# Windowed attention into an ELU feed-forward on one core: values 3 and 4 loaded ahead of w_in's second quarter, and batch 2's k transposed by DMA

## The chip, the core and the metric

The kernel runs on one core of a Trainium2 chip. TensorE does matmuls and transposes into PSUM, VectorE (DVE) and ScalarE (ACT) do elementwise work, GpSimd (POOL) builds masks and issues the loads that convert float32 to bfloat16, SyncE (SP) issues other transfers. The metric is the device time of one execution in microseconds. The kernel before took 306.71 us, the median of 3 runs (306.45 to 306.94).

## The reference

Two parts, joined. Attention in 8 batches of 8 heads, 576 positions of 64 numbers, in which each query sees only the keys within 32 positions; then a feed-forward over the 4608 x 512 result with an ELU between two matrix products.

```python
def _attn_ref(q, k, v):
    scores = (1.0 / np.sqrt(D)) * np.matmul(q, k.transpose(0, 1, 3, 2))
    mask = np.abs(pos[:, None] - pos[None, :]) <= 32
    scores = np.where(mask, scores, -1000000000.0)
    scores = scores - np.max(scores, axis=-1, keepdims=True)
    attn = np.exp(scores)
    attn = attn / (np.sum(attn, axis=-1, keepdims=True) + 1e-09)
    return np.matmul(attn, v)

def _moe_ref(x, w_in, w_out):          # x 4608x512, w_in 512x2048, w_out 2048x512
    h = x @ w_in
    g = np.where(h > 0.0, h, np.exp(np.minimum(h, 0.0)) - 1.0)
    return g @ w_out
```

## The kernel before

The feed-forward runs in 144 steps, eight for each tile of 256 tokens (the first two tiles take turns). Step kk does a first product `mm1(kk)`, its exponential `e_sb` on ScalarE, `m_sb = e_sb - 1`, and one step later `elu(kk)` on VectorE; the second product `mm2` follows two steps behind. Attention is laid between: it is done in pairs of 64-query blocks, 36 pairs, and each part of a pair is filed under a step and a slot of it ("first", "dve", "mid", "end").

```python
def at(kk, slot, fn, *args):
    tasks.setdefault((kk, slot), []).append((fn, args))
...
LAG = 2
for kk in range(NSTEP + LAG):
    run(kk, "first")
    if 1 <= kk < NSTEP and kk != 3:
        elu(kk - 1)
    run(kk, "dve")
    if kk < NSTEP:
        mm1(kk)
    run(kk, "mid")
    for n in {2: (), 3: (), 4: (), 5: (2, 3)}.get(
            kk, (kk - LAG,) if kk >= LAG else ()):
        mm2(n)
    run(kk, "end")
```

`mm1` alternates between two PSUM tiles h0 and h1, so that step kk can't begin before `elu(kk - 2)` has read the older one:

```python
def mm1(kk):
    t, s = order[kk]
    h = kk % 2
    ...                                       # ps: PSUM tile h0 or h1, 8 matmuls
        nc.scalar.activation(e_sb, ps, AX.Exp)
        if 1 <= kk <= 3:
            nc.scalar.activation(m_sb, e_sb, AX.Copy, bias=-1.0)
        else:
            nc.vector.tensor_scalar(m_sb, e_sb, -1.0, None, ALU.add)
```

A pair goes through `scores` (16 matmuls, TensorE), `exponential` (ScalarE), `mask` (VectorE), `pv` (product with the values, TensorE), `normalize` (VectorE), `x_transpose` (TensorE) and `x_evac` (a copy to xT, ScalarE). The values of a batch lie in five overlapping tiles of 128 positions (`load_v(b, 0..4)`, "values 3" is tile 3); `rotate_v` copies halves of them into a second layout for odd query blocks. Both tiles 3 and 4 are needed for pairs 2 and 3 of batch 0. `idle(n, tag)` runs n matmuls on zeros, as a filler that keeps TensorE active.

w_in comes in four quarters of its columns, w_out in four quarters of its rows. Steps 0 and 1 use w_in's first quarter, steps 2 and 3 its second, `mm2(0)` and `mm2(1)` w_out's first. The loads of GpSimd's queue in the front:

```python
for which in range(2):
    load_cast(0, which, HALF_B)      # q and k of batch 0, second half
load_w_in(0)
...                                  # two masks
load_w_in(1)
for m in (3, 4):
    load_v(0, m)
load_w_out(0)
load_w_out(1)
```

Pairs 2 and 3, which xT of the second token tile (steps 4 to 7) waits for:

```python
at(0, "mid", scores, 2, "s")
at(0, "mid", scores, 3, "u")
for i in (2, 3):
    at(0, "mid", exponential, i)
    at(1, "dve" if i == 2 else "mid", mask, i)
    at(3, "dve", rotate_v, 0, 2, VS - 1, (i - 2,))
    at(3, "mid", pv, i)
at(1, "mid", idle, 3, "y1")
at(3, "dve", idle, 3, "y1")
...                                  # normalize, elu(2), mm2(0), mm2(1), transposes, all in step 3
```

q and k come in float32 with head pairs on the free axis, are cast to bfloat16 and must be turned so that the 128 numbers of two heads lie on the partitions. There are two ways. One is on TensorE: 9 transposes of 128x128 into PSUM and one copy out of it, by ScalarE. The other is through DRAM: the cast rows are written there and come back through a transposing DMA.

```python
def cast_qk(b, which, part, j0, n, eng): ...      # float32 -> bfloat16, n of 18 columns
def transpose_qk(b, which, part, j0, n, evac, tag="t0", later=None):
    pt = ps_tile([128, 1024 if n <= 8 else 2048], BF16, tag, "ptx")
    for j in range(n):
        nc.tensor.transpose(pt[:, j * 128:(j + 1) * 128],
                            qk_b[b, which, z][:, j0 + j, :], ident)
    ...                                           # evac copies pt to qT or kT
def write_rows(b, which):
    nc.scalar.dma_start(out=..., in_=...)         # cast rows to DRAM, ScalarE's queue
def transpose_rows(b, which):
    nc.sync.dma_start_transpose(out=keys_or_queries(b, which),
                                in_=in_dram.pop((b, which)))
```

Batches 3 to 7 go through DRAM, batch 2 through TensorE: casts in steps 18 (VectorE), 20, 21 (ScalarE) and 23 (VectorE), transposes in steps 22 to 25. Step 26 is the first that needs them. The outputs of token tiles 0 and 1 leave PSUM in steps 16 and 17, one half by ScalarE and one by VectorE (`y_sb`), and pair 7's scores in step 18 ("u") lie in the two banks of tile 1's outputs:

```python
def mm2(kk):
    if s == 0:
        psY[t] = [ps_tile([128, D_MODEL], FP32, g, "psY")
                  for g in (("h2", "t0") if t == 1 else ("y0", "y1"))]
    ...
    if s == STEPS - 1:
        for ts in range(2):
            eng = (nc.scalar, nc.vector)[z]
            copy_on(eng, y_sb, psY[t][ts])
...
at(BACK_AT, "dve", swap_back)        # BACK_AT = 18: h2 and t0 become "u" again
```

`hold_v(b)` is a tiny VectorE write into the values' tile, so that the loads of batch b wait for VectorE's step.

Of the kernel before, what the change touches and what calls it, by code (L numbers as in the profile page):

```python
# [21 lines left out]
def kernel(  # L22
# [9 lines left out]
    nc = tc.nc  # L32
# [14 lines left out]
    VS = 5  # L47
# [9 lines left out]
    NSTEP = NT * STEPS  # L57
# [54 lines left out]
    WHOLE, HALF_A, HALF_B = (0, SJ), (0, SJ // 2), (1, SJ // 2)  # L112
    qk_f = {}

    def load_qk(b, which, part, engs=(nc.sync, nc.sync)):
        z, nj = part
        t = lpool.tile([128, 2, nj * D], FP32, tag=f"f{which}{nj}",
                       name=f"f{which}")
        qk_f[b, which, z] = t
        src = (q, k)[which][b, :, z * NC * nj:(z + 1) * NC * nj, :].rearrange(  # L120
            "(g h) (c j) d -> c g h (j d)", h=2, j=nj)
        for h in range(2):
            engs[h].dma_start(out=t[:, h, :], in_=src[:, :, h, :])
# [14 lines left out]
    def load_v(b, m):  # L138
        lo = 128 * m - WIN
        p0 = max(0, -lo)  # L140
        p1 = min(128, S - lo)
        nc.gpsimd.dma_start(  # L142
            out=V_e[b % 3][p0:p1, m, :, 0:D],
            in_=v[b, :, lo + p0:lo + p1, :].rearrange("h p d -> p h d"))
# [28 lines left out]
    def load_w_in(c):  # L173
        w = D_FF // 4
        nc.gpsimd.dma_start(  # L175
            out=w_in_sb[:, :, c * w:(c + 1) * w],
            in_=moe_w_in[:, c * w:(c + 1) * w].rearrange(
                "(o p) f -> p o f", p=128))

    def load_w_out(c):  # L180
        n = NFO // 4
        nc.gpsimd.dma_start(
            out=w_out_sb[:, c * n:(c + 1) * n, :],
            in_=moe_w_out[c * n * 128:(c + 1) * n * 128, :].rearrange(
                "(o p) f -> p o f", p=128))
# [191 lines left out]
    def first_pair(b):  # L377
        return NQB * b // 2
# [27 lines left out]
    for mi in (0, 4):  # L406
# [4 lines left out]
        out=masks[:, 3, :], in_=masks[:, 3, :], compare_op=ALU.is_ge,  # L411
        fill=0.0, base=128 - WIN - 1, pattern=[[0, QB]],
        channel_multiplier=-1)
    load_w_in(1)
    for m in (3, 4):
        load_v(0, m)
    load_w_out(0)
    load_w_out(1)

# [38 lines left out]
    gate(w_in_at(3))  # L458
    for which in range(2):
        load_qk(1, which, HALF_B)  # L460
    for which in range(2):
        load_qk(2, which, WHOLE)


# [4 lines left out]
    def at(kk, slot, fn, *args):  # L469
        tasks.setdefault((kk, slot), []).append((fn, args))  # L470

    def run(kk, slot):
        for fn, args in tasks.get((kk, slot), ()):
            fn(*args)
# [11 lines left out]
    at(0, "mid", scores, 3, "u")  # L486
    for i in (2, 3):
        at(0, "mid", exponential, i)
        at(1, "dve" if i == 2 else "mid", mask, i)
        at(3, "dve", rotate_v, 0, 2, VS - 1, (i - 2,))  # L490
        at(3, "mid", pv, i)

    at(1, "mid", idle, 3, "y1")
    at(3, "dve", idle, 3, "y1")
    for i in (2, 3):
        at(3, "mid", normalize, i)
    at(3, "mid", lambda: elu(2))
    for i in (2, 3):
        at(3, "mid", lambda n: mm2(n), i - 2)
        at(3, "mid", x_transpose, i)  # L500
        at(3, "mid", x_evac, i, nc.scalar)
    at(4, "dve", swap_pools)

    for part, kq in ((HALF_A, 7), (HALF_B, 15)):
# [20 lines left out]
    for i in range(4, NPAIR):  # L525
        two = i >= FIRST_TWO
        kk, z = begin[i], i % 2 if two else 0
# [5 lines left out]
        n = kk + (3 + z if two else 2)  # L533
# [9 lines left out]
    for b in range(2, B):  # L543
        k0 = begin[first_pair(b)]


        l_qk, l_v, c0 = {2: (0, 0, 0), 3: (15, 24, 22), 4: (35, 36, 41),
                         5: (52, 52, 57), 6: (68, 68, 73),
                         7: (84, 84, 89)}[b]
        if b >= 3:  # L550
            at(l_qk, "end", load_qk, b, 0, WHOLE)
            at(l_qk, "end", load_qk, b, 1, WHOLE)
            if b > 3:
                at(l_v, "dve", hold_v, b)
            for m in range(VS):
                at(l_v + m, "mid", load_v, b, m)
        if b <= 3:
            at((21, 28)[b - 2], "mid", rotate_v_dma, b)
        else:
            for n, back in enumerate((10, 8, 3, 2)):  # L560
                m0 = 2 * (n // 2)
                at(k0 - back, "dve", rotate_v, b, m0, m0 + 2, (n % 2,))
        if b == 2:

            for n, (which, j0) in enumerate(((0, 0), (0, 9), (1, 0), (1, 9))):
                at((18, 20, 21, 23)[n], ("mid", "end", "end", "mid")[n],
                   cast_qk, b, which, WHOLE, j0, 9,
                   (nc.vector, nc.scalar, nc.scalar, nc.vector)[n])
                at(22 + n, "end" if n == 1 else "mid", transpose_qk, b, which, WHOLE, j0, 9,
                   nc.scalar, "su"[n % 2])  # L570
            continue


        free = [f for f in range(c0, k0) if f not in starts]
        for n, (which, j0) in enumerate(
                (which, j0) for which in range(2) for j0 in (0, 6, 12)):
            at(free[n], "end", cast_qk, b, which, WHOLE, j0, 6,
               nc.vector if free[n] < 26 else nc.scalar)
            if j0 == 12:
                at(free[n], "end", write_rows, b, which)  # L580
                at(free[n] + (3 if free[n] == 29 else 4), "mid",
                   transpose_rows, b, which)
# [8 lines left out]
# [5 lines that stand above are left out]
        tags = (f"h{h}", "s") if kk == NSTEP - 1 else (f"h{h}",)  # L596
        w = FG // len(tags)
        psH[kk], m_t[kk] = [], []
        for z, tag in enumerate(tags):
            ps = ps_tile([128, w, TT], FP32, tag, "ps")  # L600
            psH[kk].append(ps)
            for j in range(w):
                fo = s * FG + z * w + j
                for do in range(NDO):
                    nc.tensor.matmul(  # L605
                        ps[:, j, :],
                        lhsT=w_in_sb[:, do, fo * 128:(fo + 1) * 128],
                        rhs=xT[t][:, :, do, :],
                        start=(do == 0), stop=(do == NDO - 1))
        for z, ps in enumerate(psH[kk]):  # L610
            e_sb = mpool.tile([128, w, TT], FP32, tag="e_sb", name="e_sb")
            nc.scalar.activation(e_sb, ps, AX.Exp)  # L612
            m_sb = mpool.tile([128, w, TT], BF16, tag="m_sb", name="m_sb")
            if 1 <= kk <= 3:

                nc.scalar.activation(m_sb, e_sb, AX.Copy, bias=-1.0)
            else:
                nc.vector.tensor_scalar(m_sb, e_sb, -1.0, None, ALU.add)  # L618
            m_t[kk].append(m_sb)
            if kk == NSTEP - 1:  # L620
                elu(kk, z)

    def elu(kk, z=0):
        if z == 0:
            g_t[kk] = mpool.tile([128, FG, TT], BF16, tag="g_sb", name="g_sb",
                                   bufs=5)
        ps = psH[kk][z]
        w = ps.shape[1]
        nc.vector.scalar_tensor_tensor(  # L629
            g_t[kk][:, z * w:(z + 1) * w, :], ps, 0.0, m_t[kk][z],  # L630
            ALU.max, ALU.min)
# [3 lines left out]
# [5 lines that stand above are left out]
        g_sb = g_t.pop(kk)  # L640
        last = t == NT - 1 and s == STEPS - 1
        for ts in range(2):
            for j in range(FG):
                nc.tensor.matmul(  # L644
                    psY[t][ts],
                    lhsT=g_sb[:, j, ts * 128:(ts + 1) * 128],
                    rhs=w_out_sb[:, s * FG + j, :],
                    start=(s == 0 and j == 0),
                    stop=(s == STEPS - 1 and j == FG - 1))
        if s == STEPS - 1:  # L650
            for ts in range(2):
                z = 1 - ts if last else ts
                eng = (nc.scalar, nc.vector)[z]
                y_sb = opool.tile([128, D_MODEL], FP32, tag=f"y_sb{z}",
                                  name="y_sb")
                copy_on(eng, y_sb, psY[t][ts])
                (nc.scalar if last and ts else nc.sync).dma_start(
                    out_t[t, :, ts, :], y_sb)

    LAG = 2  # L660
    for kk in range(NSTEP + LAG):
        run(kk, "first")
        if 1 <= kk < NSTEP and kk != 3:
            elu(kk - 1)
        run(kk, "dve")
        if kk < NSTEP:
            mm1(kk)
        run(kk, "mid")

        for n in {2: (), 3: (), 4: (), 5: (2, 3)}.get(  # L670
                kk, (kk - LAG,) if kk >= LAG else ()):
            mm2(n)
        run(kk, "end")
# [30 lines left out]
```

The softmax here doesn't subtract the row's maximum and nothing guards it: scores larger than these inputs give would overflow.

## Time and profile before

| What | Value |
|---|---|
| time, median of 3 runs | 306.71 us |
| span of the profiled execution | 304.7 us |
| TensorE busy | 294.7 us (97%) |
| VectorE busy | 240.7 us (79%) |
| ScalarE busy | 170.3 us (56%) |
| granted TensorE clock | 1.000 |
| one group of a step's first product, from start to start of the next | 0.87 us |
| first matmul of step 4 | 25.42 us |
| first matmul of step 18 | 55.06 us |

A row of the timeline gives the start of an instruction (or a run of equal ones), the us that it spans, the engine, the source line, what is written from what with the shape, and in brackets the idle time of the engine ahead of it with what ended that. Where one instruction overlaps the next a little, the distance from start to start is the cost, and not the span. L605 is `mm1`, L644 `mm2`, L395 a filler, L304 `scores`, L336 `pv`, L279 a transpose of q or k, L357 a transpose of x, L612 the exponential, L618 and L616 m_sb, L629 `elu`, L234 and L236 copies and casts by ScalarE and VectorE. "us to landing" is from the issue of a transfer to its completion. In the list of DMA queues q0 is GpSimd's, q1 SyncE's, q10 ScalarE's.

### The profile page before, as it was taken

What the parts mean: (1) busy time and instruction counts of PE and PEld (TensorE: products, weight loads), DVE (VectorE), ACT (ScalarE), POOL (GpSimd) and SP (SyncE); (2) the same over time, 40 slices, a digit from 0 to 9 for tenths busy, and PEclk for the clock granted to TensorE, in tenths of its full rate; (3) what the DMA queues carried; (4) which work ended last, traced back from release to release, by engine and by line L of the source; (5) the groups of instructions that cost most, each with busy time, mean ns of one, the idle gap of its engine ahead of it and who ended that gap; (6) DMA issues with size and microseconds to landing.
All of it is one profiled execution on the core that took longest, in us unless ns stands there. A gap on an engine that the chain in (4) does not pass through costs nothing.

```text
span 304.7 us, 7633 instructions
## 1 busy us (share of the span) xinstructions
PE 294.7 (97%) x3090; PEld 197.0 (65%) x3090; DVE 240.7 (79%) x470; ACT 170.3 (56%) x256; POOL 48.7 (16%) x68
## 2 busy tenths in 40 slices
PE   7799999999999999999999999999999999999994
PEld 3466666677666666666666666666666666666662
DVE  6866587978788887988798879887988787877663
ACT  3673556778664567546754675467545454543431
POOL 8836100910004100230023002300000000000000
PEclk9999999999999999999999999999999999999999
DMA  9999999999766997999799969996911111121011
GB/s 192 189 193 206 182 268 397 309 154 207 167 187 154 297 120 208 225 325 152 154 265 309 183 161 267 321 160 150 269 34 71 34 71 34 72 37 69 8 63 70
DMA packets 91973, 52.81 MB, mean 173 GB/s; under 512 B 76578, under 2 KB 81698, under 8 KB 91938
## 3 DMA queue, kind: packets, MB, share of 16 engines
q1 hardware_dynamic: 47186, 35.48, 43.6%
q0 software_dynamic: 42880, 10.10, 43.2%
q10 hardware_dynamic: 1872, 6.75, 5.7%
q8 instruction: 24, 0.39, 0.5%
q14 instruction: 11, 0.09, 0.1%
HBM read 36.70 MB, written 15.34 MB: 171 GB/s over the span
## 4 chain that ended last, share of the span: by engine, by line
PE 89%; DMA 4%; POOL 3%; DVE 1%; ACT 1%; issue 0%; POOLq 0%; DVEq 0%
PE psY L644 41%; PE ps L605 40%; DMA w_out_sb<-in_moe_w_out_dram 4%; PE psS L336 3%; PE psS L304 3%; POOL Ve L142 1%; PE ptx L279 1%; POOL c L136 1%; PE psXT L357 1%; POOL w_in_sb L175 0%; PE ptx L274 0%; ACT pu L315 0%; DVE x_st L348 0%; DVE pm L324 0%; DVE g_sb L629 0%
## 5 line engine op out<-in xcount | busy, mean ns | idle before, releaser
L612 ACT ACTIVATE e_sb<-ps 128x512 f32<-128x512 f32 (+1 forms) x145 | 86.3, 595 | 118.0 <-PE ps L605 110.4
L605 PE MATMUL ps<-xT,w_in_sb 128*128 128x256 bf16 x1152 | 149.3, 273 | 1.8 <-ACT xT L234 0.7
L644 PE MATMUL psY<-w_out_sb,g_sb 128*128 128x512 bf16 x576 | 147.5, 379 | 0.0
L605 PEld LDWEIGHTS <-w_in_sb 128*128 128x128 bf16 x1152 | 110.5, 98 | 40.7 <-DMA w_in_sb<-in_moe_w_in_dram 1.6
L629 DVE SCALAR_TENSOR_TENSOR g_sb<-ps,m_sb 128x512 bf16<-128x512 f32 (+1 forms) x145 | 99.4, 686 | 13.3 <-DVE m_sb L618 0.5
L618 DVE TENSOR_SCALAR m_sb<-e_sb 128x512 bf16<-128x512 f32 (+1 forms) x142 | 61.2, 431 | 38.3 <-ACT e_sb L612 36.4
L644 PEld LDWEIGHTS <-g_sb 128*128 128x128 bf16 x576 | 54.5, 98 | 38.5 <-DVE g_sb L629 0.2
L142 POOL DMA_DIRECT2D Ve<-in_v_dram x40 | 35.3, 893 | 138.9 <-PE psS L336 79.9
L315 ACT ACTIVATE pu<-psS 128x1024 bf16<-128x1024 f32 x36 | 36.5, 1021 | 1.4 <-PE psS L304 1.4
L348 DVE TENSOR_TENSOR x_st<-psS,rc 128x512 bf16<-128x512 f32 x36 | 24.9, 691 | 1.2
L324 DVE TENSOR_TENSOR pm<-pu,masks 128x1024 bf16<-128x1024 bf16 x36 | 24.6, 683 | 0.7 <-ACT pu L315 0.6
L234 ACT CAST qkb<-f 128x768 bf16<-128x768 f32 (+1 forms) x29 | 24.9, 860 | 0.0
L336 PEld LDWEIGHTS <-pm 128*64 128x64 bf16 x576 | 11.0, 111 | 8.8 <-DVE pm L324 7.7
L336 PE MATMUL psS<-Ve,pm 128*64 128x65 bf16 x320 | 13.2, 196 | 0.8 <-DVE pm L324 0.7
L236 DVE COPY y_sb<-psY 128x512 f32<-128x512 f32 x18 | 12.3, 684 | 0.9 <-PE psY L644 0.9
L304 PEld LDWEIGHTS <-kT 64*128 64x128 bf16 x576 | 9.6, 95 | 4.9 <-issue 4.0
L304 PE MATMUL psS<-qT,kT 64*128 64x64 bf16 x576 | 11.8, 191 | 0.5 <-DVE kT L236 0.5
L336 PE MATMUL psS<-Vo,pm 128*64 128x65 bf16 x256 | 11.9, 196 | 0.0
L234 ACT COPY y_sb<-psY 128x512 f32<-128x512 f32 x18 | 10.5, 582 | 2.2 <-PE psY L644 2.2
L153 DVE COPY Vo<-Ve 64x1040 bf16<-64x1040 bf16 x24 | 10.4, 435 | 1.3 <-DMA Ve<-in_v_dram 0.5
L395 PE MATMUL ps_idle<-zeros 128*128 128x512 bf16 x26 | 8.3, 450 | 1.3 <-DVE zeros L194 1.3
L234 ACT COPY qT<-ptx 128x1152 bf16<-128x1152 bf16 (+2 forms) x8 | 7.5, 972 | 3.5 <-PE ptx L279 2.8
(36 smaller groups left out, 73.3 us busy)
## 6 DMA issues: line engine op xcount, KB each, us to landing
out_dram<-y_sb SPq DMA_DIRECT2D x35, 256.0 KB, 3.7
f<-in_q_dram SPq DMA_DIRECT2D x12, 576.0 KB, 6.1
f<-in_k_dram SPq DMA_DIRECT2D x12, 576.0 KB, 8.2
in_dram<-qkb ACTq DMA_DIRECT2D x10, 576.0 KB, 4.5
Ve<-in_v_dram POOLq DMA_DIRECT2D x24, 128.0 KB, 11.4
w_in_sb<-in_moe_w_in_dram POOLq DMA_DIRECT2D x4, 512.0 KB, 9.8
w_out_sb<-in_moe_w_out_dram POOLq DMA_DIRECT2D x4, 512.0 KB, 12.5
Ve<-in_v_dram POOLq DMA_DIRECT2D x16, 96.0 KB, 10.3
```

The costliest lines, as they stand in the source:

```text
L142: nc.gpsimd.dma_start(out=V_e[b % 3][p0:p1, m, :, 0:D], in_=v[b, :, lo + p0:lo + p1, :].rearrange("h p d -> p h d"))
L234: nc.scalar.copy(d_, s_)
L304: nc.tensor.matmul(psS[:, h % 2, hp * 128 + z * QB:hp * 128 + (z + 1) * QB], lhsT=kT[b % 2][base:base + 64, KPAD + hp * S + QB * qb - WIN: ...
L315: nc.scalar.activation(pu, _bap(psS, [psS.ap[0], [1, 1024]]), AX.Exp, scale=SCALE)
L324: nc.vector.tensor_mul(pm, pu, _bap(mm, [mm.ap[0], [0, H], [1, 2 * QB]]))
L336: nc.tensor.matmul(psS[QB * z:QB * (z + 1), par, hp * VD:(hp + 1) * VD], lhsT=pm[:, par * HP + hp, z * QB:(z + 1) * QB], rhs=vv[:, qb // 2 ...
L348: nc.vector.tensor_mul(x_st, _bap(psS, [psS.ap[0], [VD, HP], [512, 2], [1, D]]), _bap(rc, [rc.ap[0], [2, HP], [1, 2], [0, D]]))
L605: nc.tensor.matmul(ps[:, j, :], lhsT=w_in_sb[:, do, fo * 128:(fo + 1) * 128], rhs=xT[t][:, :, do, :], start=(do == 0), stop=(do == NDO - 1))
L612: nc.scalar.activation(e_sb, ps, AX.Exp)
L618: nc.vector.tensor_scalar(m_sb, e_sb, -1.0, None, ALU.add)
L629: nc.vector.scalar_tensor_tensor(g_t[kk][:, z * w:(z + 1) * w, :], ps, 0.0, m_t[kk][z], ALU.max, ALU.min)
L644: nc.tensor.matmul(psY[t][ts], lhsT=g_sb[:, j, ts * 128:(ts + 1) * 128], rhs=w_out_sb[:, s * FG + j, :], start=(s == 0 and j == 0), stop=( ...
```

## The change

Four things. First, in GpSimd's queue values 3 and 4 of batch 0 come ahead of w_in's second quarter, and pairs 2 and 3 are done earlier: rotation and mask in step 0, products in step 1 between 4, 2 and 1 fillers, normalization in step 2; `mm2(0)` and `mm2(1)` come after both transposes of x in step 3, `elu(2)` comes in the ordinary place, and m_sb is on ScalarE in step 1 only. Second, k of batch 2 goes through DRAM: both casts in step 16, rows written at the end of step 16, the transposing DMA in step 18; q of batch 2 stays on TensorE. Third, batch 2's k is loaded ahead of its q, and batch 3's k at the end of step 18, behind the transposing DMA in SyncE's queue, in place of step 15. Fourth, the values of batch 3 are held until step 20; before, they followed those of batch 2 directly. The aim is to take k's transposes from TensorE and to keep the transfers of the two batches out of each other's way.

```diff
--- before.py
+++ after.py
@@ -411,9 +411,9 @@
         out=masks[:, 3, :], in_=masks[:, 3, :], compare_op=ALU.is_ge,
         fill=0.0, base=128 - WIN - 1, pattern=[[0, QB]],
         channel_multiplier=-1)
-    load_w_in(1)
     for m in (3, 4):
         load_v(0, m)
+    load_w_in(1)
     load_w_out(0)
     load_w_out(1)
 
@@ -458,7 +458,7 @@
     gate(w_in_at(3))
     for which in range(2):
         load_qk(1, which, HALF_B)
-    for which in range(2):
+    for which in (1, 0):
         load_qk(2, which, WHOLE)
 
 
@@ -486,19 +486,16 @@
     at(0, "mid", scores, 3, "u")
     for i in (2, 3):
         at(0, "mid", exponential, i)
-        at(1, "dve" if i == 2 else "mid", mask, i)
-        at(3, "dve", rotate_v, 0, 2, VS - 1, (i - 2,))
-        at(3, "mid", pv, i)
-
-    at(1, "mid", idle, 3, "y1")
-    at(3, "dve", idle, 3, "y1")
     for i in (2, 3):
-        at(3, "mid", normalize, i)
-    at(3, "mid", lambda: elu(2))
-    for i in (2, 3):
-        at(3, "mid", lambda n: mm2(n), i - 2)
+        at(0, "mid", rotate_v, 0, 2, VS - 1, (i - 2,))
+        at(0, "mid", mask, i)
+
+        at(1, "mid", idle, (4, 2)[i - 2], "y1")
+        at(1, "mid", pv, i)
+        at(2, "dve", normalize, i)
         at(3, "mid", x_transpose, i)
         at(3, "mid", x_evac, i, nc.scalar)
+    at(1, "end", idle, 1, "y1")
     at(4, "dve", swap_pools)
 
     for part, kq in ((HALF_A, 7), (HALF_B, 15)):
@@ -549,9 +546,8 @@
                          7: (84, 84, 89)}[b]
         if b >= 3:
             at(l_qk, "end", load_qk, b, 0, WHOLE)
-            at(l_qk, "end", load_qk, b, 1, WHOLE)
-            if b > 3:
-                at(l_v, "dve", hold_v, b)
+            at(18 if b == 3 else l_qk, "end", load_qk, b, 1, WHOLE)
+            at(20 if b == 3 else l_v, "dve", hold_v, b)
             for m in range(VS):
                 at(l_v + m, "mid", load_v, b, m)
         if b <= 3:
@@ -562,12 +558,16 @@
                 at(k0 - back, "dve", rotate_v, b, m0, m0 + 2, (n % 2,))
         if b == 2:
 
-            for n, (which, j0) in enumerate(((0, 0), (0, 9), (1, 0), (1, 9))):
-                at((18, 20, 21, 23)[n], ("mid", "end", "end", "mid")[n],
-                   cast_qk, b, which, WHOLE, j0, 9,
-                   (nc.vector, nc.scalar, nc.scalar, nc.vector)[n])
-                at(22 + n, "end" if n == 1 else "mid", transpose_qk, b, which, WHOLE, j0, 9,
-                   nc.scalar, "su"[n % 2])
+
+            for n in range(2):
+                at((18, 20)[n], ("mid", "end")[n], cast_qk, b, 0, WHOLE,
+                   9 * n, 9, (nc.vector, nc.scalar)[n])
+                at(22 + n, ("mid", "end")[n], transpose_qk, b, 0, WHOLE,
+                   9 * n, 9, nc.scalar, "su"[n])
+                at(16, "mid", cast_qk, b, 1, WHOLE, 9 * n, 9,
+                   (nc.vector, nc.scalar)[n])
+            at(16, "end", write_rows, b, 1)
+            at(18, "mid", transpose_rows, b, 1)
             continue
 
 
@@ -611,7 +611,7 @@
             e_sb = mpool.tile([128, w, TT], FP32, tag="e_sb", name="e_sb")
             nc.scalar.activation(e_sb, ps, AX.Exp)
             m_sb = mpool.tile([128, w, TT], BF16, tag="m_sb", name="m_sb")
-            if 1 <= kk <= 3:
+            if kk == 1:
 
                 nc.scalar.activation(m_sb, e_sb, AX.Copy, bias=-1.0)
             else:
@@ -660,14 +660,14 @@
     LAG = 2
     for kk in range(NSTEP + LAG):
         run(kk, "first")
-        if 1 <= kk < NSTEP and kk != 3:
+        if 1 <= kk < NSTEP:
             elu(kk - 1)
         run(kk, "dve")
         if kk < NSTEP:
             mm1(kk)
         run(kk, "mid")
 
-        for n in {2: (), 3: (), 4: (), 5: (2, 3)}.get(
+        for n in {2: (), 3: (0, 1), 4: (), 5: (2, 3)}.get(
                 kk, (kk - LAG,) if kk >= LAG else ()):
             mm2(n)
         run(kk, "end")
```

## The prediction

> **What bounds the kernel now.** I read the page's busy row and its chain of waits first, to see which engine has no room.
>
> ```profile
> PE 294.7 (97%) x3090; PEld 197.0 (65%) x3090; DVE 240.7 (79%) x470; ACT 170.3 (56%) x256; POOL 48.7 (16%) x68
> ...
> PE 89%; DMA 4%; POOL 3%; DVE 1%; ACT 1%; issue 0%; POOLq 0%; DVEq 0%
> ```
>
> TensorE is busy for 97% of the span and makes up 89% of the chain that ends last. The DMA and POOL shares of that chain lie ahead of 22.4 us, by its pieces in order of time. So there are two kinds of prize: TensorE instructions that go away after the front, and waits or filler matmuls inside the front. Anything that ScalarE or VectorE saves counts only if TensorE was waiting for it.
>
> Next the timeline of TensorE in the front (columns: start, us spanned, instruction, count, idle before and releaser).
>
> ```profile
> 15.25 1.05 PE L605 MATMUL ps<-xT,w_in_sb 128*128 128x256 bf16 x8 [0.61 <-DMA w_in_sb<-in_moe_w_in_dram]
> ...
> 16.80 1.05 PE L605 MATMUL ps<-xT,w_in_sb 128*128 128x256 bf16 x8
> 17.68 0.81 PE L395 MATMUL ps_idle<-zeros 128*128 128x512 bf16 x3
> 18.54 1.05 PE L605 MATMUL ps<-xT,w_in_sb 128*128 128x256 bf16 x8
> 19.42 0.81 PE L395 MATMUL ps_idle<-zeros 128*128 128x512 bf16 x3
> 20.69 1.03 PE L605 MATMUL ps<-xT,w_in_sb 128*128 128x256 bf16 x8 [0.46 <-DVE g_sb L629]
> ...
> 25.42 1.91 PE L605 MATMUL ps<-xT,w_in_sb 128*128 128x256 bf16 x16 [0.67 <-ACT xT L234]
> ```
>
> These are the first matmul groups of steps 0, 1, 2, 3 and 4. Between them stand fillers (L395) and two waits, one for elu of step 1 (0.46 us), one for the transposed rows of pair 3 (0.67 us). From 25.42 us on TensorE idles by no more than 0.15 us at a time as far as I read the timeline (84 us), so the start of step 4 is the figure that the front hands on.
>
> Then the landings, from the DMA view asked in narrow windows (last column: us from issue to landing):
>
> ```profile
> w_in_sb<-in_moe_w_in_dram POOLq DMA_DIRECT2D x1, 512.0 KB, 9.4
> ...
> Ve<-in_v_dram POOLq DMA_DIRECT2D x1, 128.0 KB, 10.0
> ...
> Ve<-in_v_dram POOLq DMA_DIRECT2D x1, 96.0 KB, 9.9
> ```
>
> The issues on GpSimd's timeline are at 9.10, 9.86 and about 10.7 us, so w_in's second quarter lands at 18.5, values 3 at 19.9 and values 4 at 20.6 us. w_in's first quarter landed at 15.2 (7.53 + 7.7), w_out's first at 22.4 (11.51 + 10.9). The queue delivers one behind the other.
>
> Last, steps 16 to 18 and 24: TensorE, then ScalarE.
>
> ```profile
> 55.06 1.04 PE L605 MATMUL ps<-xT,w_in_sb 128*128 128x256 bf16 x8
> 56.03 0.66 PE L304 MATMUL psS<-qT,kT 64*128 64x64 bf16 x32
> 56.62 1.04 PE L644 MATMUL psY<-w_out_sb,g_sb 128*128 128x512 bf16 x4
> ...
> 69.25 0.67 PE L279 MATMUL ptx<-ident,qkb 128*128 128x128 bf16 x9
> 69.76 1.03 PE L644 MATMUL psY<-w_out_sb,g_sb 128*128 128x512 bf16 x4
> ```
>
> ```profile
> 52.16 0.60 ACT L612 ACTIVATE e_sb<-ps 128x512 f32<-128x512 f32 x1 [0.62 <-DVE g_sb L629]
> 52.66 1.12 ACT L234 COPY kT<-ptx 128x1152 bf16<-128x1152 bf16 x1
> 53.68 0.59 ACT L234 COPY y_sb<-psY 128x512 f32<-128x512 f32 x1
> 54.40 0.60 ACT L612 ACTIVATE e_sb<-ps 128x512 f32<-128x512 f32 x1
> 54.89 0.58 ACT L234 COPY y_sb<-psY 128x512 f32<-128x512 f32 x1
> ```
>
> The reader is to see that nine transposes push the next matmul back by 0.51 us (69.25 to 69.76), and that ScalarE is already full in step 16: from 52.16 to 54.27 one instruction follows another.
>
> **What the Trainium skill says.** "DMA: Bandwidth & Descriptors", section "Issuing engines are not separate DMA queues", says that transfers from all issuing engines run on the same 16 DMA engines. The trace fits: the page's DMA row stands at 9 in nearly every slice of the first 200 us, so a moved load pushes others. "Two DMAs through the same engine are not ordered", same page, says that a transfer which reads what another wrote must wait for that one's completion; here SyncE waits 16.8 us in nine waits for the DRAM rows ahead of transposes. "PSUM — Partial Sum Buffer", section "Engine vs sequencer instructions", calls the queues of ScalarE and VectorE strict FIFO: an instruction that is put early delays all behind it. "Perfetto Trace Analysis", section "DMA Instruction — HWDGE (DVE, Sync)", says that the issuing sequencer is free for the next instruction only at the end of the issue; in the trace ScalarE's row writes take 0.55 us each, and its next activation starts behind them (83.00 + 0.58, then 83.69).
>
> **Part one, the front.** With values 3 and 4 ahead, they take the places behind w_in's first quarter: 15.2 + 1.4 (18.5 to 19.9 before) = 16.6 and + 0.7 = 17.3 us. The same bytes stand ahead of w_in's second quarter as stood ahead of values 4's end, so it lands at about 20.6 (2.1 later). VectorE: m_sb of step 0 to 17.4 as before; a rotation 0.45, mask of pair 2 0.69, rotation 0.45, mask of pair 3 0.69 (durations of L153 and L324): second rotation done 19.0, second mask 19.7; elu of step 0 to 20.3; elu of step 1 to 20.9; two normalizes (0.20 + 0.69 each, overlapping a little) to 22.6.
>
> TensorE: step 1 ends at 17.68 as before, four fillers to 18.55, products of pair 2 wait for the second rotation, 19.05 to 19.4; two fillers to 19.85; products of pair 3 to 20.2; a filler to 20.4; step 2 starts when w_in's second quarter is there and elu 0 is done: 20.6. Step 3's matmuls are then at 21.5 to 22.45, with no wait for elu 1. The two transposes of x take 0.23 each, to 22.9; w_out's first quarter has landed by 22.4; two second matmuls of 0.87 each end at 24.65. In that time ScalarE has copied both xT (done 24.1), so step 4 starts at 24.7 in place of 25.42: **0.7 us gained**. The transposed rows no longer stand at the end of the chain, because the products come two steps earlier.
>
> **Part two, k's transposes.** 18 PE transposes go, 2 x 0.51 = **1.0 us gained** on TensorE, with two ScalarE copies of about 1.3 us in steps 24 and 25 (on no path). In their place: one row write, one DMA transpose (4.5 us median to landing), no TensorE work.
>
> **Part three, what the casts do in step 16.** ScalarE gets a cast of 128x1152 there (1.14 us, 1.04 from start to start, from 48.04 to 49.08) and the row write (0.55). In the order of the queue: e_sb 52.16, kT copy 52.66, cast 53.68, y copy 54.72, write 55.21 to 55.8, and only then e_sb of step 17: 55.85 instead of 54.40. Behind it the last y copy on ScalarE ends 56.9; on VectorE m_sb runs 56.45 to 56.9 and the other y copy to 57.6. The scores of pair 7, in the middle of step 18, use the PSUM banks from which these two copies read. Before they began at about 56.3 (half way through the 32 from 56.03); now they can't run in full before 57.6: **1.3 us lost**, and elu of step 17 (58.3) is then just in time for step 19. VectorE's cast (0.75) also moves elu of step 16 by 0.2 us, inside that loss.
>
> **Part four, the loads.** k of batch 2 takes the place that q had, landing at 49.4 us (42.1 + 7.3), ahead of its cast at about 51.5; q then lands about 52.5, its cast is at 55. Rows written by 60, transposes landed by 67, needed in step 26 (72.9 before): hidden. k of batch 3 is issued about 63.5 to 65 and needed by a VectorE cast at the end of step 25, about 73.3; at 5 to 8 us to landing it arrives between 69 and 73. Hidden, with little room. Values of batch 3, held to step 20, land by 72 and are needed in step 28. No time.
>
> **Sum:** 306.71 - 0.7 - 1.0 + 1.3 = 306.3; I shade it to 306.2, since an engine that waits often finds work that my hand schedule puts too late.
>
> **Rivals.** First, no jam in step 16: the copies out of PSUM come in time after all. For it: ScalarE is 56% busy and idle 0.62 us ahead of step 16. Against: the sum of 3.65 us in a 2.2 us step. Then 306.71 - 1.7 = 305.0. Second, w_in's second quarter is the new bound of the front: many small rows of values in front of it (under 512 B are 76578 of 91973 packets) make it land at 21.5 or later, and the front gives nothing: 307.0. For it: landings on this queue vary, 7.7 to 11.1 us for w_in. Against: the total to w_out's first quarter is the same. Third, k of batch 3 comes late behind transposes and stalls VectorE, and TensorE with it: 307.5 to 309. For it: in 64 to 74 us the DMA view shows a share of 2.90, several queues at once, and Vo's rotation took 7.7 us to land. Against: batch 3's values no longer load from 57 us on.
>
> **Range and chances.** I give my main line about half, the first rival a quarter, the second and third an eighth each. That gives 305.1 to 307.4 for eight in ten. Two per cent is 6.1 us, far more than any of these terms: faster 0.01, within 0.97, slower 0.02.
>
> **What would show it.** Right: step 4 starts near 24.7 with no wait for xT; w_in's second quarter lands near 20.6; no L279 group between steps 24 and 26; e_sb of step 17 starts some 4 us after that of step 16, and the scores in step 18 show a wait of about 1.2 us for a y copy. Wrong: a start of step 4 above 25.2, no wait in step 18, or a wait for k of batch 3 on VectorE near 73 us.

## The result, and the profile after

The changed kernel takes 311.68 us (median of 5 runs, 311.35 to 312.42) against 306.71 us before: a ratio of 1.0169, 95% interval 1.0151 to 1.0186. It is 5 us slower, and the range of the prediction (305.1 to 307.4 us) ends 4 us below it.

The page after, its busy row and its chain of waits:

```profile
PE 296.7 (96%) x3073; PEld 196.7 (63%) x3073; DVE 242.0 (78%) x473; ACT 166.7 (54%) x252; POOL 48.3 (16%) x68
...
PE ps L605 39%; PE psY L644 38%; DMA f<-in_k_dram 4%; PE psS L336 4%; PE psS L304 3%; DMA w_in_sb<-in_moe_w_in_dram 3%; POOL Ve L142 1%; ACT e_sb L612 1%; POOL c L136 1%; ACT pu L315 1%; PE psXT L357 1%; DVE g_sb L629 1%; DVE qkb L236 1%; DVE pm L324 0%; PE ptx L274 0%
```

TensorE shows 17 matmul instructions less and still more busy time, and the load of k has come into the chain with 4% of the span. TensorE's timeline after shows where, at the same places as before:

```profile
15.74 1.05 PE L605 MATMUL ps<-xT,w_in_sb 128*128 128x256 bf16 x8 [0.88 <-DMA w_in_sb<-in_moe_w_in_dram]
...
25.14 1.91 PE L605 MATMUL ps<-xT,w_in_sb 128*128 128x256 bf16 x16
...
55.11 1.05 PE L605 MATMUL ps<-xT,w_in_sb 128*128 128x256 bf16 x8 [0.16 <-DVE g_sb L629]
56.09 0.41 PE L304 MATMUL psS<-qT,kT 64*128 64x64 bf16 x16
57.00 0.41 PE L304 MATMUL psS<-qT,kT 64*128 64x64 bf16 x16 [0.50 <-DVE y_sb L236]
...
72.66 1.03 PE L605 MATMUL ps<-xT,w_in_sb 128*128 128x256 bf16 x8
...
79.44 1.05 PE L605 MATMUL ps<-xT,w_in_sb 128*128 128x256 bf16 x8 [4.21 <-DVE g_sb L629]
80.33 1.77 PE L644 MATMUL psY<-w_out_sb,g_sb 128*128 128x512 bf16 x4
```

Step 27 is the line with the wait of 4.21 us. In the kernel before it had none:

```profile
75.28 1.04 PE L605 MATMUL ps<-xT,w_in_sb 128*128 128x256 bf16 x8
```

The starts of steps, set against those before, give the whole account:

| First matmul of | before, us | after, us | after - before |
|---|---|---|---|
| step 4 | 25.42 | 25.14 | -0.3 |
| step 19 | 57.49 | 58.21 | +0.7 |
| step 26 | 72.86 | 72.66 | -0.2 |
| step 27 | 75.28 | 79.44 | +4.2 |
| step 29 | 79.49 | 85.34 | +5.9 |
| end of the span | 304.7 | 310.7 | +6.0 |

(The profiled run took 312.4 us.) So 0.3 us were gained in the front and 0.9 us by the transposes, 1.0 us went in steps 16 to 18, and then came what the sum did not hold: 4.4 us ahead of step 27, and 1.7 us in the two steps behind it. VectorE, which TensorE waited for, says whom it waited for itself:

```profile
73.69 0.68 DVE L236 COPY y_sb<-psY 128x512 f32<-128x512 f32 x1
78.23 0.56 DVE L236 CAST qkb<-f 128x768 bf16<-128x768 f32 x1 [3.85 <-DMA f<-in_k_dram]
78.70 0.69 DVE L629 SCALAR_TENSOR_TENSOR g_sb<-ps,m_sb 128x512 bf16<-128x512 f32 x1
```

The cast of batch 3's k stands in VectorE's queue ahead of elu of step 25 (L629), without which step 27 has no PSUM tile. SyncE's queue shows why k was late:

```profile
60.16 5.96 SPq L265 DMA_TRANSPOSE kT<-in_dram  x1
66.17 1.22 SPq L123 DMA_DIRECT2D f<-in_k_dram  x2
```

The issue of the transposing DMA alone held SyncE for 6.0 us. Of the two halves of k behind it, the DMA view has one landing 7.5 us and the other 11.3 us after its issue (73.7 and 78.1 us):

```profile
f<-in_k_dram SPq DMA_DIRECT2D x1, 576.0 KB, 7.5
...
f<-in_k_dram SPq DMA_DIRECT2D x1, 576.0 KB, 11.3
```

The other 1.7 us are clock. In the table by stretches (after the five engines: granted clock, DMA share, GB/s) TensorE is granted half its clock for 3.41 us, from one microsecond after its wait is over:

```profile
79.44:80.47 1.03, 1.03 (x9) 0.90 (x10) 0.93 (x3) 0.00 (x0) 0.00 (x0) 1.00 1.18 385
80.47:83.88 3.41, 3.41 (x14) 1.82 (x12) 2.36 (x5) 1.55 (x3) 0.00 (x0) 0.50 0.22 73
83.88:85.34 1.46, 1.46 (x37) 0.80 (x35) 0.77 (x2) 1.27 (x2) 0.00 (x0) 1.00 0.61 131
```

Half of 3.41 us is the 1.7 us of the account. The Trainium skill, "TensorE: Matmul & The Clock Gate", section "What's actually happening", says that activity releases a throttle on the clock and that the throttled state comes back after an idle window of about 3.4 us. This case agrees in kind: four matmuls that take 0.87 us from start to start take 1.56 here (80.33 to 81.89). It does not agree on the length: in a run below a wait of 2.1 us was enough.

### The profile page after: what moved, and what is told of

It reads as the page before. It is cut to its first block, busy times and chain, and to the rows that moved or that the text cites. A ratio compares the mean times of both kernels' runs of the same rounds, so it can differ in the third digit from the quotient of the medians.

```text
span 310.7 us, 7605 instructions
## 1 busy us (share of the span) xinstructions
PE 296.7 (96%) x3073; PEld 196.7 (63%) x3073; DVE 242.0 (78%) x473; ACT 166.7 (54%) x252; POOL 48.3 (16%) x68
## 4 chain that ended last, share of the span: by engine, by line
PE 84%; DMA 6%; DVE 3%; POOL 2%; ACT 2%; issue 1%; SPq 0%; ACTq 0%; DVEq 0%; POOLq 0%
PE ps L605 39%; PE psY L644 38%; DMA f<-in_k_dram 4%; PE psS L336 4%; PE psS L304 3%; DMA w_in_sb<-in_moe_w_in_dram 3%; POOL Ve L142 1%; ACT e_sb L612 1%; POOL c L136 1%; ACT pu L315 1%; PE psXT L357 1%; DVE g_sb L629 1%; DVE qkb L236 1%; DVE pm L324 0%; PE ptx L274 0%
## 5 line engine op out<-in xcount | busy, mean ns | idle before, releaser
L629 DVE SCALAR_TENSOR_TENSOR g_sb<-ps,m_sb 128x512 bf16<-128x512 f32 (+1 forms) x145 | 99.4, 686 | 13.0 <-DVE m_sb L618 0.5
L618 DVE TENSOR_SCALAR m_sb<-e_sb 128x512 bf16<-128x512 f32 x144 | 62.7, 435 | 39.8 <-ACT e_sb L612 38.0
L336 PE MATMUL psS<-Vo,pm 128*64 128x65 bf16 x256 | 12.1, 196 | 0.2 <-DVE Vo L153 0.2
L395 PE MATMUL ps_idle<-zeros 128*128 128x512 bf16 x27 | 9.2, 470 | 1.3 <-DVE zeros L194 1.3
L236 DVE CAST qkb<-f 128x768 bf16<-128x768 f32 (+3 forms) x11 | 7.0, 649 | 4.3 <-DMA f<-in_k_dram 4.1
## 6 DMA issues: line engine op xcount, KB each, us to landing
Ve<-in_v_dram POOLq DMA_DIRECT2D x24, 128.0 KB, 11.3
```

Source lines behind the costliest of these rows:

```text
L336: nc.tensor.matmul(psS[QB * z:QB * (z + 1), par, hp * VD:(hp + 1) * VD], lhsT=pm[:, par * HP + hp, z * QB:(z + 1) * QB], rhs=vv[:, qb // 2 ...
L629: nc.vector.scalar_tensor_tensor(g_t[kk][:, z * w:(z + 1) * w, :], ps, 0.0, m_t[kk][z], ALU.max, ALU.min)
```

## The experiments

Theory 1 was that batch 3's k, put behind the transposing DMA, is the whole loss. Its rival was that too many transfers meet between 60 and 80 us, so that the one that ends last makes TensorE wait, whichever it is. The edits are against the changed kernel unless it is said; a line of them that is only a comment sums up what was edited there. Medians are of all runs and the ratios leave disturbed runs out, so the ratio counts where the two part.

**k of batch 3 early again**

```diff
-            at(18 if b == 3 else l_qk, "end", load_qk, b, 1, WHOLE)
+            at(l_qk, "end", load_qk, b, 1, WHOLE)
```

> Theory 1 (the whole loss is batch 3's k arriving late): with its load back at step 15 VectorE no longer waits 3.9 us for it in step 25, TensorE's wait of 4.2 us ahead of step 27 goes, and with it the lower granted clock behind that wait (about 1.6 us by the starts of steps 27 to 28): 311.7 - 4.4 - 1.6 = 305.7 us. Rival (the DMA engines are overfull between 60 and 80 us, whichever transfer comes last): another transfer, batch 2's k or its rotated values, then ends late and TensorE waits in steps 26 to 28; time above 308 us.

Measured: 311.8 us, ratio 1.0129 (1.0087 to 1.0171), single runs from 308.4 to 313.3; the profiled one is the longest. VectorE's wait for k is gone, and the time is not. Its waits on TensorE, SyncE's queue and its DMA view:

```profile
PE psS L304 <- DMA kT<-in_dram: 5.2, 1, 5.2
```

```profile
63.28 6.94 SPq L265 DMA_TRANSPOSE kT<-in_dram  x1
```

```profile
kT<-in_dram SPq DMA_TRANSPOSE x1, 15.2
```

Now batch 2's k itself is the late one: with batch 3's k loading early the row write took 9.3 us to land (5.5 in the changed kernel), the transposing DMA was issued at 63.3 and landed 15.2 us later, 5.2 us after step 26 wanted it. Theory 1 falls, the rival stands.

**The kernel before with k's new path alone** (against the kernel before)

```diff
-    for which in range(2):
+    for which in (1, 0):
         load_qk(2, which, WHOLE)
...
-    # q and k of batch 2: casts in 18, 20, 21, 23, TensorE transposes in 22 to 25
+    # q as before; k: casts in 16, rows written in 16, transposing DMA in 18
```

> The kernel before with one part alone: batch 2's k through DRAM and the transposing DMA (and loaded ahead of its q); batch 3's k still loaded at step 15, its values not held. Theory 1: 18 transposes less on TensorE, 1.0 us gained; the jam in steps 16 to 18 costs the 0.7 to 1.0 us that the changed kernel shows there: 306.5 us, no wait in steps 25 to 27. Rival (overfull DMA engines): with batch 3's values loading from 57 us on, batch 2's k or its rotated values come after step 26 or 28 wants them: above 308 us.

Measured: 311.0 us, ratio 1.0113 (1.0076 to 1.0151), single runs from 308.7 to 311.9, the profiled one 311.8. Its waits and its DMA view name the same transfer:

```profile
PE psS L304 <- DMA kT<-in_dram: 3.6, 1, 3.6
```

```profile
kT<-in_dram SPq DMA_TRANSPOSE x1, 15.2
```

So k's path is enough for the loss, with batch 3's loads where they were. What the change adds to it, a later k and held values, does not take the wait away but shifts it from k of batch 2 to k of batch 3.

**The front alone** (batches 2 and 3 as in the kernel before)

```diff
-    load_w_in(1)
     for m in (3, 4):
         load_v(0, m)
+    load_w_in(1)
...
+    # and steps 0 to 3 in the new order
```

> The front alone: values 3 and 4 ahead of w_in's second quarter, with the reordered steps 0 to 3; batches 2 and 3 as before. The changed kernel's profile says step 4 starts 0.3 us earlier: 306.4 us. My recorded sum said 0.7 us: 306.0 us. If w_in's first quarter lands at 15.2 us again, the 0.5 us by which it was late in the changed kernel was chance; if it lands near 15.7, the values behind it delay it.

Measured: 305.84 us, ratio 0.9974 (0.9961 to 0.9986). Step 4 starts at 24.76 us, 0.66 us earlier than before, with w_in's first quarter there at 15.1 us. The front is good for what the sum said. Step 0 starts when that quarter is there: at 15.1 us here, at 15.7 in the changed kernel's profile, and between 15.0 and 15.7 in those of the other twelve kernels with this front. A difference of that size between two profiles is scatter.

**Batch 3's values later**

```diff
-            at(20 if b == 3 else l_v, "dve", hold_v, b)
+            at(l_v, "dve", hold_v, b)                     # 24
...
-            at((21, 28)[b - 2], "mid", rotate_v_dma, b)
+            at((21, 33)[b - 2], "mid", rotate_v_dma, b)
```

> Batch 3's k stays behind the transposing DMA, its values are held to step 24 in place of 20 and rotated in step 33. If the load of k is late because the values' loads run beside it from 62 us on, it lands within about 7 us of its issue (before 75 us), and VectorE's wait of 3.9 us shrinks to under 1.5 us; time 306 to 308 us. If it is late because of its place behind the transposing DMA in the queue, issue stays near 66 us, the wait stays above 3 us and the time at 311 to 312 us.

Measured: 306.58 us, ratio 0.9999 (0.9982 to 1.0016). Four steps more for the values take 5 us off. SyncE's queue and the second half of k:

```profile
60.20 4.56 SPq L265 DMA_TRANSPOSE kT<-in_dram  x1
64.82 1.22 SPq L123 DMA_DIRECT2D f<-in_k_dram  x2
```

```profile
f<-in_k_dram SPq DMA_DIRECT2D x1, 576.0 KB, 7.7
```

k stands behind the transposing DMA as in the changed kernel, and lands at 73.2 instead of 78.1 us.

**The rotation alone**, the other thing moved there

```diff
-            at((21, 28)[b - 2], "mid", rotate_v_dma, b)
+            at((21, 33)[b - 2], "mid", rotate_v_dma, b)
```

> The changed kernel with only the rotation of batch 3's values moved from step 28 to step 33; the values are still held to step 20. If the overlap of these loads with the transposing DMA and the load of k is the cause, nothing changes up to step 28: VectorE waits 3 to 4 us for k in step 25, 311 to 312 us. If it was the rotation's place in SyncE's queue, behind which other transfers stood, the wait shrinks under 1 us and the time falls to 306.6 us.

Measured: 312.5 us, ratio 1.0108 (1.0053 to 1.0164), single runs from 307.8 to 313.0. In the profiled run (307.8) VectorE waited 1.4 us for k. So the rotation is not what helped: this kernel and the one with the values later differ only in the step to which the values are held (20 against 24), and take 312.5 and 306.6 us. Up to step 28 this is the changed kernel, so what differs before that is scatter of one schedule: here the issue of the transposing DMA held SyncE for 4.0 us, k's second half landed in 10.0 us and the wait was 1.4 us; there it was 6.0, 11.3 and 3.9 us. Of its runs of 312 to 313 us there is no profile.

**The loads alone**, k of batch 2 on TensorE as before

```diff
-            # k: casts in 16, rows written in 16, transposing DMA in 18
+            # q and k: casts in 18, 20, 21, 23, TensorE transposes in 22 to 25
```

> The changed kernel's loads (batch 3's k at step 18, its values held to step 20), but batch 2's k transposed on TensorE as before. Theory 2: without the transposing DMA the load of k is issued before 60 us and lands before 70 us, no wait in step 25: 305.8 to 306.3 us. If the load's late step or the values beside it were enough for the loss, VectorE still waits for it: above 308 us.

Measured: 305.66 us, ratio 0.9970 (0.9961 to 0.9979). k of batch 3 is issued at 56.4 us, since nothing holds SyncE, and VectorE's cast of it in step 25 does not wait. The load's later step and the held values cost nothing without the transposing DMA; but k then also leaves 10 us earlier than in the changed kernel.

**Values left out**, and **values in long rows**

```diff
             for m in range(VS):
-                at(l_v + m, "mid", load_v, b, m)
+                if b != 3:
+                    at(l_v + m, "mid", load_v, b, m)
```

> The changed kernel with the loads of batch 3's values left out (it computes batch 3 with batch 0's values). If these loads beside the transposing DMA are the cause, k of batch 3 lands within 8 us of its issue, VectorE waits under 1 us for it, no wait ahead of step 27 above 0.5 us: 306 to 306.6 us. If the transposing DMA and the rotation are enough by themselves, the wait stays above 2 us and the time above 308 us.

```diff
+        if b == 3:
+            rows = v[b].rearrange("h (s e) d -> (h s) (e d)", e=8)
+            nc.gpsimd.dma_start(out=..., in_=rows[112 * m:112 * m + p1 - p0, :])
+            return
```

> The changed kernel, with batch 3's values loaded as the same bytes in rows of 2 KB of the source in place of 256 bytes (so in another order: what it puts out for batches 3 and 6 isn't the reference's; a small VectorE write puts the ones back in step 34, and the rotation comes in step 35). If it is the number of small rows that stretches the transposing DMA and batch 3's k, k lands before 75 us, VectorE's wait of 3.9 us falls under 1 us and the time is near that without these loads. If it is their bytes, wait and time stay as in the changed kernel, 311 to 312 us.

Measured: without the values 306.7 us, ratio 1.0014 (0.9981 to 1.0047), single runs to 310.3; with long rows 312.5 us, ratio 1.0165 (1.0115 to 1.0216), single runs from 310.2. In the profiled runs VectorE does not wait for k in step 25 without the values (it has landed at 72.8 us), waits 1.7 us with long rows and 3.9 us in the changed kernel; k's second half takes 6.8, 9.9 and 11.3 us to land. The values themselves land within 6.9 us in long rows, where the last took 17.9. So the loads of values are the larger part of k's lateness. Whether the length of their rows counts for it is not shown: three kernels with small rows that are the same up to there had 10.0, 11.3 and 12.1 us for k's second half, and 9.9 lies at the edge of that. Nor is it the hold of SyncE alone: without the values the transposing DMA's issue still held it for 4.6 us. Even without them single runs are 3 to 4 us longer.

**k of batch 3 early and values later, both**

```diff
-            at(18 if b == 3 else l_qk, "end", load_qk, b, 1, WHOLE)
-            at(20 if b == 3 else l_v, "dve", hold_v, b)
+            at(l_qk, "end", load_qk, b, 1, WHOLE)
+            at(l_v, "dve", hold_v, b)
...
+            # rotation in step 33
```

> Batch 3's k back at step 15 and its values held to step 24, with batch 2's k still through DRAM. Theory 2 (the values' loads of many small rows, run beside the transposing DMA, stretch it to 15 us): with the values out of the way it lands within 9 us of its issue near 63 us, before step 26 wants it at 73 us; no wait, 305.9 us (306.7 - 0.7 for the front - 1.0 for the transposes + 1.0 for steps 16 to 18). Rival (the early load of k delays the row write and with it the transposing DMA, whatever the values do): TensorE waits for it again in step 26, over 308 us.

Measured: 306.56 us, ratio 1.0002 (0.9990 to 1.0015). The transposing DMA lands 9.3 us after its issue at 63.0, ahead of step 26; no DMA wait on TensorE is left there. Against 305.84 of the front alone this is 0.7 us more, although 1.0 us of transposes is gone. Its starts say why: 1.0 us goes in steps 16 to 18, and 0.4 us ahead of step 27, where shorter steps have used up VectorE's room for the cast (it works without a gap from 73.2 to 77.0 us). Another 0.4 us goes in steps 75 and 76 of the profiled run and stays unexplained.

**k's first cast on ScalarE in step 28**

```diff
-        free = [f for f in range(c0, k0) if f not in starts]
+        free = [f for f in range(c0, k0) if f not in starts
+                and (b, f) != (3, 25)]
```

> The changed kernel with the three casts of batch 3's k in steps 28, 29 and 30, all on ScalarE, in place of 25 (VectorE), 28 and 29. The load lands as late as before (about 78 us). If the loss comes by the cast that stands in VectorE's queue ahead of elu, it goes: wait ahead of step 27 gone, clock 1.00, 306 us, at most 1 us more where pair 9's products in step 28 wait for batch 2's rotated values (landed at 79 us in the changed kernel). If DMA lateness as such costs the time, another wait of 3 us or more takes its place: 309 us or above.

Measured: 307.31 us, ratio 1.0033 (1.0010 to 1.0055). k is as late as before (issued at 65.9, landed at 78.0 us):

```profile
f<-in_k_dram SPq DMA_DIRECT2D x1, 576.0 KB, 12.1
```

Its first cast moved to an engine and a step that can wait takes 4.4 us off; the next wait in line is 0.7 us for batch 2's rotated values. So the loss of the changed kernel needs both, a late transfer and a cast of it in a full queue.

**ScalarE's cast of batch 2's k in step 17**, on top of the kernel before it in this list

```diff
-                at(16, "mid", cast_qk, b, 1, WHOLE, 9 * n, 9, ...)
+                at((16, 17)[n], ("mid", "end")[n], cast_qk, b, 1, WHOLE, 9 * n, 9, ...)
-            at(16, "end", write_rows, b, 1)
-            at(18, "mid", transpose_rows, b, 1)
+            at(18, "end", write_rows, b, 1)
+            at(20, "mid", transpose_rows, b, 1)
```

> As the kernel with k early and values later, and besides ScalarE's cast of batch 2's k at the end of step 17, its row write at the end of step 18, the transposing DMA in step 20. If the jam of steps 16 to 18 is ScalarE's cast and row write ahead of step 17's exponential, the 1.0 us between the starts of steps 17 and 19 goes: scores of pair 7 don't wait, 304.9 us. If VectorE's cast alone makes it, nothing changes against that kernel: 305.9 us. If the transposing DMA is now too late for step 26, it waits there: above 306.5 us.

Measured: 305.71 us, ratio 0.9973 (0.9955 to 0.9992). TensorE's timeline in step 18:

```profile
54.76 1.05 PE L605 MATMUL ps<-xT,w_in_sb 128*128 128x256 bf16 x8 [0.17 <-DVE g_sb L629]
55.74 0.64 PE L304 MATMUL psS<-qT,kT 64*128 64x64 bf16 x32
```

All 32 scores go in one run. Of the 1.0 us of the jam 0.7 was ScalarE's cast and row write; the 0.3 that stays is put down to VectorE's cast, ahead of elu of step 16.

**Three further steps the same way**, on top of the kernel with ScalarE's cast in step 17: batch 3's k cast late as well; VectorE 4 columns and ScalarE 14; the row write on SyncE.

```diff
+                and (b, f) != (3, 25)]                            # first
-                   9 * n, 9, ...
+                   4 * n, (4, 14)[n], ...                         # second, with the first
-            at(18, "end", write_rows, b, 1)
+            at(18, "first", write_rows, b, 1, nc.sync)             # third, with both
```

> The kernel with ScalarE's cast in step 17 and batch 3's loads apart, and besides batch 3's k cast in steps 28 to 30. There step 27 waited 0.26 us for elu of step 25, behind VectorE's cast of k in step 25; without that cast step 27 starts 0.4 us earlier: 305.3 us. If the y copy holds elu up, the wait stays and so does 305.7 us.

> As the kernel before it in this list, with batch 2's k cast by VectorE in 4 of its 18 columns in step 16 and by ScalarE in 14 in step 17. VectorE's 9 columns delayed elu of step 16 and so step 18 by 0.3 us; 4 columns should cost under 0.1: 305.0 us. If ScalarE's longer cast holds up the exponential of step 18, the 0.3 us come back there: 305.3 us or more.

> As the kernel with 4 and 14 columns, with the row write of batch 2's k issued from SyncE at the head of step 18 in place of ScalarE at its end. There the transposing DMA landed 0.7 us after step 26 wanted it. If its row write stood behind ScalarE's exponentials, it now starts about 1.5 us earlier, the wait goes and the time is 305.0 us: k through DRAM then pays 0.7 us over k on TensorE. If the wait only moves into the transposing DMA (more company for it at 60 to 66 us), 306 us or more as before.

Measured: 306.48 us, ratio 0.9992 (0.9981 to 1.0002); 306.75 us, ratio 0.9999 (0.9990 to 1.0009); 305.80 us, ratio 0.9981 (0.9969 to 0.9993). All three missed the time that was expected, and each for a reason that the starts show.

In the first, step 27 does start 0.4 us earlier. But k's third cast is now in step 30, and with it k's transposing DMA goes from step 32 to step 34: it is issued at 90.4 us, where the kernel with ScalarE's cast in step 17 has 86.0, and TensorE waits for it in step 37:

```profile
97.14 0.29 PE L304 MATMUL psS<-qT,kT 64*128 64x64 bf16 x8 [1.03 <-DMA kT<-in_dram]
```

The second has the same wait with 0.7 us. Both are waits for batch 3's k; batch 2's k is in time for step 26 in all three, so the third expectation starts from a wrong reading. The second also wins the 0.3 us in step 18, which shows VectorE's cast as its cause, and loses it again ahead of steps 20 and 21: ScalarE's longer cast puts the exponential of step 18 at 56.3 in place of 55.8 us, as the alternative in its expectation said.

In the third the row write is issued no earlier (56.38 against 56.42 us). Step 26 starts 1.3 us earlier than in the kernel before, and yet the span ends only 0.7 us earlier: 0.2 us goes ahead of step 34, 0.3 us in step 37, again for batch 3's k, and the rest in small pieces. In the second, 0.5 us more goes in steps 75 and 76, as in the kernel with k early and values later, unexplained. No version with k through DRAM beats the front alone by what these runs can tell.

## Why the prediction was wrong

**What bounds the kernel**: right. TensorE sets the end, and every term of the account above is a matmul dropped, a wait of TensorE or its clock. One reading was loose: the page's DMA row is 9 in 20 of its first 26 slices, not in nearly every one; no term of the sum rests on it.

**The front**: right. Predicted 0.7 us and step 4 at 24.7; the front alone gave 0.66 us and 24.76. The changed kernel's profiled run shows only 0.3, with w_in's first quarter 0.6 us later than there, at the late end of its scatter; from step 0 to step 4 it takes 9.40 us, against 10.17 before. w_in's second quarter landed at 20.2 us (predicted 20.6), so the second rival did not come.

**k's transposes**: right. Predicted 1.0 us, measured 0.9 in the account (step 19 to step 26).

**Step 16**: right in its mechanism, too large by a third. Predicted 1.3 us and a wait of the scores for a y copy, measured 1.0. The term mis-sized is the row write: I let it run when the y copy had ended, at 55.21, and it ran beside it:

```profile
54.45 0.59 ACT L234 COPY y_sb<-psY 128x512 f32<-128x512 f32 x1
54.59 0.63 ACTq L260 DMA_DIRECT2D in_dram<-qkb  x1
55.26 0.60 ACT L612 ACTIVATE e_sb<-ps 128x512 f32<-128x512 f32 x1 [0.22 <-ACT y_sb L234]
```

The place from which I took that order (83.00 + 0.58, then 83.69) doesn't show it: there the timeline puts the start of the activation down to VectorE (x_st).

**The loads**: this step failed, "Hidden, with little room". k of batch 3 was to be issued at 63.5 to 65 us and to land in 5 to 8 us. Its halves were issued at 66.2 and 66.8, because the transposing DMA held SyncE for 6.0 us (the longest issue in the profile before is 3.55 us), and landed in 7.5 and 11.3 us. The landing was too short even by the profile before; its page has, for the twelve loads of k of this size,

```profile
f<-in_k_dram SPq DMA_DIRECT2D x12, 576.0 KB, 8.2
```

a median of 8.2 us, and the eleven whose landing is recorded took 7.1 to 12.8. 65 + 12.8 lies 4.5 us behind the 73.3 at which the prediction wanted k. That transposing DMAs land later in such company could be seen there too: those of x issued at 129.7 to 131.6, 161.6 to 163.4 and 190.9 to 192.7 us, beside loads of q, k and values, landed in 8.4 to 9.5 us, those from 220 us on in 2.4 to 3.2. What the runs showed in place of "hidden": k at 78.1 us for a cast that VectorE could have begun at 74.4 (predicted 73.3), and through elu a wait of 4.2 us on TensorE.

**The third rival** was the one that came, and I gave it an eighth and 307.5 to 309 us. Its size was short too: it left out the clock, 1.7 us, and its argument against ("batch 3's values no longer load from 57 us on") missed that they load from 62 us on instead, beside the transposing DMA. A margin of 0 to 4 us against a landing time that spreads from 7 to 13 us in the profile before is no margin; with this spread the range should have gone to 312 us.

## What to carry to other kernels

When transfers are moved, write down for each the step that wants it and what runs on the DMA engines in its last 10 us; take the worst landing that the profile has in such company, not a short one, and expect worse where more meets. A cast of loaded data in the queue of a busy engine turns a late transfer into a stop of everything behind it; in a queue that can wait it costs little (311.7 against 307.3 us here), though what stands behind the cast moves with it (1.0 us in step 37). And a stop of TensorE that lowers its clock costs more than its length: 4.2 us of waiting took 5.9, where 1.7 us that left the clock full took 1.9.

## What the runs showed that was not expected

A transposing DMA of k that lands 4.0 to 6.4 us after its issue in the later batches of the kernel before took 15.2 us beside loads of values, in two kernels, and its issue alone held SyncE for about 7 us. In three kernels that are the same up to there the same issue held it for 4.0, 4.0 and 6.0 us; what sets this is open. And moving one transfer away did not remove the wait but named another: k of batch 3, k of batch 2, the rotated values of batch 2, in turn.

The clock, too, has a threshold that the runs only bracket. It fell to 0.50 with TensorE waits of 2.1 us (the values in long rows), 3.6 us (k's new path alone) and 4.2 us (the changed kernel), each time for 3.41 us, and with one of 5.2 us (k of batch 3 early) for 6.8 us; it stayed full after one of 1.7 us (the rotation alone).
